# Causal attention and an MLP block on one NeuronCore: normalised rows of batches 2 to 5 turned by SyncE's transposing DMAs, MLP chunks begun two heads later

## The chip, the cores and the metric

The kernel runs on one core of one Trainium2 chip. The metric is the device time of one execution in microseconds. Before the change it is 359.73 us, the median of three runs (357.85 to 361.63).

## The reference

Eight batches with eight heads each, sequence 576, head size 64. First causal attention with a cumulative bias, then per row a layer norm and a two-layer MLP (512 to 2048 to 512) with a residual:

```python
scores = scale * np.matmul(q, k.transpose(0, 1, 3, 2))
s_pos = np.maximum(s, 0.0)
cum = np.cumsum(s_pos, axis=-1)
bias = -(cum[:, :, :, None] - cum[:, :, None, :])
scores = np.where(causal, -1000000000.0, scores + np.minimum(bias, 0.0))
attn = softmax(scores)                       # rows
x = np.matmul(attn, v)                       # heads side by side: (8, 576, 512)
mu, var = mean and variance of each row of x
xn = (x - mu) / np.sqrt(var + 1e-06) * g_ln
out = x + np.maximum(xn @ w_ch1, 0.0) @ w_ch2
```

## The kernel before, in words

All 64 (batch, head) pairs are numbered n = 8 b + h. TensorE computes, head by head, the transposed scores in three PSUM banks (`sa`, `sb`, `sc`, and `sd` for the last 64 rows of a pair of heads), ScalarE exponentiates them into `er`, GpSimd zeroes the part above the diagonal (`affine_select`), TensorE multiplies with the values into `pot` (`pv`, two heads behind), and VectorE divides by the row sums into `xb`, the fp32 rows of x (`pv_norm`). Rows 512 to 575 of two batches share one tile `xm`, so that an odd batch has five tiles of rows and an even one four.

Layer norm and MLP of a batch follow its attention. `ln_stats` takes the statistics in three parts as heads 3, 5 and 7 of the batch are finished; `ln_xn` writes the centred and scaled rows in bf16 (`xn`, the division by the deviation is left to the end, as `rstd`). These are turned into `xT` (features on partitions) in one of two ways. `ln_tr` has TensorE turn four 128x128 blocks into a PSUM bank of pool `ps_t` (tile `trx`), which VectorE or ScalarE copies out. `ln_tr_dma` has SyncE (SP) issue one transposing DMA from `xn` into `xT`. Constant `NXD` chooses: batches up to `NXD - 1` go through TensorE, the later ones through the DMA. Then a chunk of 32 units of MLP work is put into `queue`: 16 times `mlp1` (four matmuls of 512 columns into bank `ph`, ReLU into `hT`), and 16 times `mlp2` (four matmuls, a quarter of one row tile's output in `py`; after the fourth, VectorE writes `yo` and SP stores it). `ph` and `py` share the two PSUM banks of pool `ps_m`; the scores have three banks in `ps_s`. A ninth chunk does the shared row tiles (`xTm`).

The keys and queries of the first five groups of four heads (a group is called `gam` in the code, 0 to 15) come over other ways. From group 5 on, SP loads fp32 rows (`ld_rows`, ten transfers for a group, named `rowtmp`, line 175), GpSimd casts them into `rows`, a part of `kq[2]` (`cast_rows`, lines 192 and 195), and SP issues five transposing DMAs into `kq[0]` or `kq[1]` (`tr_rows`, line 208). `pre(n)` and `post(n)` hold the schedule: the loads of group g are placed at n = 4g-6, 4g-5 and 4g-4, the casts one head later, the transposes at 4g-4 and 4g-3, and the first use is at n = 4g. The values are loaded with a cast by GpSimd's own DMA queue (`ld_cast_v`). `pre(14)` has GpSimd write zeroes into columns 68 to 127 of the five `rows` tiles.

The order is written out by hand (`manual_schedule`): every engine runs its instructions in the order in which the program records them, and waits in it. SP's queue thus holds, in one line, row loads, transposes of keys and queries, transposes of `xn`, and stores of `yo`; a store that waits for its `yo` holds up everything recorded after it. The main loop (n = 18 to 63) records for each head its scores, one MLP unit, `post`, another unit, a finished head's `pv_next`, the layer norm steps of the batch before, and further units so that the chunk is used up by `end`, the head after which the next chunk is put in.

Of the kernel before, what the change touches and what calls it, by code (L numbers as in the profile page):

```python
# [9 lines left out]
F32 = mybir.dt.float32  # L10
# [5 lines left out]
P = 128  # L16
# [3 lines left out]
def kernel(  # L20
# [11 lines left out]
    nc = tc.nc  # L32
    B, H, S, D = q.shape
# [5 lines left out]
    NF = S // P  # L39
# [9 lines left out]
    NPE = 5  # L49
    NM = 10  # L50
    NHW = 16
    NXD = 6
    KT = 96
    QT = 6
    QP = S // QT
# [282 lines left out]
    def scores(b, h):  # L338
        e = er[:, h % 4, :]
        pe_mask = b * H + h < NM  # L340

        def bank(name, blocks, o):
            a = ps_s.tile([P, 512], F32, name=name, tag="s")
            for c, kb, q0, q1, diag in blocks:
                for a0, a1, cols in q_cols(b, h, q0, q1):
                    nc.tensor.matmul(  # L346
                        a[:, c + a0 - q0 : c + a1 - q0],
                        lhsT=k_cols(b, h, kb),
                        rhs=cols,
                        start=True,  # L350
                        stop=not (pe_mask and diag),
                    )
                if pe_mask and diag:
                    nc.tensor.matmul(
                        a[:, c : c + P], lhsT=ident, rhs=maskT, start=False, stop=True
                    )
            nc.scalar.activation(out=e[:, o : o + 512], in_=a, func=ACT.Exp, scale=scale)  # L357

        bank("sa", ((0, 0, 0, 512, True),), 0)
        bank("sb", ((0, 0, 512, 576, False), (64, 1, 128, 576, True)), OB)  # L360
        bank("sc", ((0, 2, 256, 576, True), (320, 3, 384, 576, True)), OC)
        if pe_mask:
            return
        for o, step in ((0, OB + 64), (OC, 320)):
            two = e[:, o : o + 2 * step].rearrange("p (i c) -> p i c", c=step)[:, :, 0:P]
            nc.gpsimd.affine_select(  # L366
                out=two,
                in_=two,
                compare_op=ALU.is_ge,
                fill=0.0,  # L370
                base=0,
                pattern=[[0, 2], [1, P]],
                channel_multiplier=-1,
            )
# [78 lines left out]
        return ts_  # L453

    st = {}

    def ln_stats(b, part):
        if part == 0:
            st[b] = small.tile([P, 5, 3, 6], F32, name="stats", tag="stats", bufs=2)
        lo, hi = ((0, 256), (256, 384), (384, 512))[part]  # L460
        for t, x in enumerate(x_tiles(b)):
            nc.vector.bn_stats(out=st[b][:, t, part, :], in_=x[:, lo:hi])  # L462

# [66 lines left out]

    def mlp1(xT, fb):
        on_dve = first_unit[0]
        ph = ps_m.tile([P, 512], F32, name="ph", tag="m")
        for kd in range(KD):
            nc.tensor.matmul(  # L537
                ph,
                lhsT=w1_bf[:, kd, fb * P : (fb + 1) * P],
                rhs=xT[:, kd, :],  # L540
                start=(kd == 0),
                stop=(kd == KD - 1),
            )
        if on_dve:
            nc.vector.tensor_scalar_max(out=hT[:, fb, :], in0=ph, scalar1=0.0)  # L545
        else:
            nc.scalar.activation(out=hT[:, fb, :], in_=ph, func=ACT.Relu)  # L547
# [22 lines left out]
    def chunk_units(xT_of, of_t, last=False):  # L570
        units = [lambda fb=fb: mlp1(xT_of(), fb) for fb in range(FB)]
        for t in range(NF):
            halves = ((0, 256), (256, 512)) if last and t == NF - 1 else ((0, 512),)
            for c in halves:
                for qr in range(4):
                    units.append(lambda t=t, qr=qr, c=c: mlp2(t, qr, *of_t(t), *c))
        return units
# [18 lines left out]
    def run_units(n, dve_first=False):  # L596
        for i in range(n):
            if queue:
                first_unit[0] = dve_first and i == 0
                queue.pop(0)()  # L600

# [24 lines left out]
    nc.vector.memset(v_bf[0][0:TL, NF, :, D : D + 1], 1.0)  # L628
    for i in range(2):
        nc.vector.memset(kq[i][0:KA, 0, :, S:SP], 0.0)  # L630
    nc.vector.memset(kq[2][0:KA, 0, :, S:SP], 0.0)
    nc.vector.memset(eight, 1.0 / scale)
    nc.vector.memset(mhalf, -0.5)
    nc.vector.memset(c3[BH:KT], 0.0)
# [22 lines left out]
    ld_cast_tile("q", NF)  # L657
    ld_cast_v(0, NF)

    for u, two in ((0, -1.0058441162109375), (1, 1.0019378662109375)):  # L660
        nc.gpsimd.memset(kq[2][D:KA, u].bitcast(F32)[:, :, 0 : S // 2], two)
    ld_w1(1)
    nc.gpsimd.memset(v_bf[1][:, 0:NF, :, D : D + 1], 1.0)
    nc.gpsimd.memset(v_bf[1][0:TL, NF, :, D : D + 1], 1.0)
# [185 lines left out]


    def pre(n):
        if n == 14:
            for r in rows:
                nc.gpsimd.memset(r[:, :, :, KA:P], 0.0)
        if n in PAIR_LOADS:
            ld_cast_pair(PAIR_LOADS[n])
        if n in (11, 12):
            ld_w2(n - 9)
        if n in (8, 9):  # L860
            aug(n - 5, nc.sync)
        for gam in range(NPE, NG):
            m = n - 4 * gam
            ts_ = {-6: (0, 1), -5: (2, 3), -4: (4,)}.get(m, ())
            for t in ts_:
                if gam < NHW:
                    ld_rows(gam, t)
                else:
                    ld_cast_rows(gam, t)
                    bias_of_rows(gam, t)  # L870
            if gam >= NHW:
                for t in {-4: (0, 1), -3: (2, 3, 4)}.get(m, ()):
                    tr_rows(gam, t)
        for nb in range(2, B):
            t = n - H * nb + (5 if nb == 2 else 6)
            if 0 <= t < NT:
                ld_cast_v(nb, t)

# [97 lines left out]
        STEPS[name](*args, *([E[eng]] if eng else []))  # L976

    pend += [(2, 0), (2, 1)]
    for n in range(2 * H + 2, BH):
        b, h = n // H, n % H  # L980
        pre(n)

        end = next(m for m in [8 * i + (3 if i <= NXD else 4) for i in range(2, B)] + [BH + 3] if m >= n)
        nu = -(-len(queue) // (end - n + 1)) - 2
        scores(b, h)
        run_units(1, True)
        if h % 2 == 0:
            scores_d(b, h // 2)
        post(n)
        run_units(1)  # L990
        pv_next()
        pend.append((b, h))
        if b <= NXD:
            if n == 2 * H + 2:
                for t in range(3, NT):
                    ln_xn(1, t)
            if b > 2 and h == 1:
                for t in range(NT):
                    ln_xn(b - 1, t)
            for t in {2: (0, 1), 3: (2, 3, 4)}.get(h, ()):  # L1000
                ln_tr(b - 1, t, "act" if b == 2 else "dve")
                if t != 1 and t != 4:
                    run_units(1)
                    nu -= 1
        elif h in (1, 2):
            for t in ((0, 1, 2), (3, 4))[h - 1]:
                ln_xn(b - 1, t)
                ln_tr_dma(b - 1, t)
                run_units(1)
                nu -= 1  # L1010
        run_units(nu)
        if n == end:
            run_units(len(queue))
            queue += batch_units(b - 1)
# [41 lines left out]
```

## Time and profile before

| | |
|---|---|
| median of three runs | 359.73 us (357.85 to 361.63) |
| the profiled execution: its own time | 358.78 us |
| its span, first to last instruction | 357.1 us |
| TensorE (PE) matmul rows busy | 349.3 us, 98% of the span |
| VectorE (DVE), ScalarE (ACT), GpSimd (POOL) busy | 196.2, 185.5, 162.2 us |
| SP's ring of the DMA queues (q1) | 116016 packets, 36.53 MB |
| granted TensorE clock | 1.000 |

A busy TensorE row holds the latency of a matmul too, and the rows of successive matmuls overlap; the rate is read from the starts of a run of them. "PEld" is the weight load, which overlaps the matmul. In the views an entry such as `[1.71 <-DMA kq<-kq]` tells how long the engine had been idle before an instruction and what released it.

### The profile page before, as it was taken

To read this page: it belongs to the slowest core of one execution; us is meant where nothing else is said; L and a number is where in the kernel's file an instruction comes from. 1 tells how busy PE (TensorE), PEld (TensorE's weight loads), DVE (VectorE), ACT (ScalarE), POOL (GpSimd) and SP (SyncE) were. 2 spreads that over 40 slices of the span, in tenths; PEclk is the share of its full clock that TensorE was granted. 3 is DMA by queue.
4 is the path that set the end of the run, shared out by engine and by line. 5 is a ranking of instruction groups with operands and counts; after the bars stand their busy time and mean duration, and the time that the engine had idled before them with its cause. 6 is when DMAs were issued, how large, how long until landed. Compare 5 with 4: busy or idle time off the path is not lost.

```text
span 357.1 us, 8417 instructions
## 1 busy us (share of the span) xinstructions
PE 349.3 (98%) x3154; PEld 198.9 (56%) x3154; DVE 196.2 (55%) x535; ACT 185.5 (52%) x359; POOL 162.2 (45%) x344
## 2 busy tenths in 40 slices
PE   8999999999899999999999999999999999999995
PEld 3899666555455555555565555555555544444444
DVE  7788888944376536844384539543764582113111
ACT  4899886577434763267336743475366403402500
POOL 9997669458436742582556452665341010000000
PEclk9999999999999999999999999999999999999999
DMA  9999999999979998699979974999740043011013
GB/s 151 170 180 171 199 190 166 191 192 168 184 147 204 153 212 149 106 226 172 171 129 213 207 145 84 222 180 174 158 119 2 0 80 113 0 61 60 0 32 89
DMA packets 169098, 49.73 MB, mean 139 GB/s; under 512 B 157744, under 2 KB 164448, under 8 KB 169056
## 3 DMA queue, kind: packets, MB, share of 16 engines
q1 hardware_dynamic: 116016, 36.53, 53.6%
q0 software_dynamic: 51600, 11.87, 37.1%
q10 hardware_dynamic: 1440, 0.79, 0.8%
q8 instruction: 25, 0.41, 0.5%
q14 instruction: 17, 0.14, 0.1%
HBM read 37.11 MB, written 9.44 MB: 130 GB/s over the span
## 4 chain that ended last, share of the span: by engine, by line
PE 84%; DVE 6%; DMA 3%; SPq 3%; POOL 2%; issue 1%; ACT 1%; DVEq 0%; POOLq 0%; ACTq 0%
PE py L555 31%; PE ph L537 29%; PE pot L424 6%; PE sc L346 3%; PE sb L346 3%; PE sa L346 3%; PE ph L817 2%; DVE xn L499 2%; DMA kq<-kq 2%; PE st L715 2%; SPq L175 1%; DMA rowtmp<-in_q_dram 1%; PE trx L526 1%; SPq L208 1%; PE pot L773 1%
## 5 line engine op out<-in xcount | busy, mean ns | idle before, releaser
L555 PE MATMUL py<-w_bf,hT 128*128 128x512 bf16 (+1 forms) x592 | 135.5, 373 | 0.4 <-DVE yo L564 0.4
L537 PE MATMUL ph<-xT,w_bf 128*128 128x512 bf16 x480 | 114.0, 379 | 0.0
L547 ACT ACTIVATE hT<-ph 128x512 bf16<-128x512 f32 x101 | 60.2, 597 | 74.3 <-PE ph L537 74.3
L555 PEld LDWEIGHTS <-hT 128*128 128x128 bf16 x592 | 53.7, 98 | 50.7 <-issue 0.9
L537 PEld LDWEIGHTS <-w_bf 128*128 128x128 bf16 x544 | 48.7, 97 | 50.5 <-issue 3.1
L366 POOL TENSOR_SCALAR_AFFINE_SELECT er<-er 128x256 bf16<-128x256 bf16 x108 | 43.7, 419 | 53.2 <-ACT er L357 52.3
L357 ACT ACTIVATE er<-sa 128x512 bf16<-128x512 f32 x56 | 33.3, 595 | 64.9 <-PE sa L346 50.3
L545 DVE TENSOR_SCALAR hT<-ph 128x512 bf16<-128x512 f32 x35 | 24.2, 692 | 57.3 <-PE ph L537 52.4
L192 POOL CAST kq<-rowtmp 128x512 bf16<-128x512 f32 (+1 forms) x55 | 33.5, 609 | 29.3 <-DMA rowtmp<-in_q_dram 27.4
L346 PEld LDWEIGHTS <-kq 68*128 68x128 bf16 x412 | 29.7, 97 | 23.5 <-DMA kq<-kq 2.0
L424 PEld LDWEIGHTS <-er 128*128 128x128 bf16 x840 | 32.8, 98 | 11.9
L436 DVE RECIPROCAL rinv<-pot 128x5 f32<-128x5 f32 x56 | 10.7, 192 | 50.0 <-PE pot L424 49.8
L564 DVE SCALAR_TENSOR_TENSOR yo<-py,rstd,xb 128x512 f32<-128x512 f32 x32 | 24.0, 749 | 24.2 <-PE py L555 19.5
L424 PE MATMUL pot<-v_bf,er 128*128 128x65 bf16 x840 | 34.7, 194 | 0.0
L165 POOL DMA_DIRECT2D v_bf<-in_v_dram x40 | 34.4, 867 | 0.3 <-DVE kq L116 0.3
L357 ACT ACTIVATE er<-sb 128x512 bf16<-128x512 f32 x56 | 33.5, 598 | 1.3 <-PE sb L346 1.3
L357 ACT ACTIVATE er<-sc 128x512 bf16<-128x512 f32 x56 | 34.1, 610 | 0.0
L478 POOL TENSOR_TENSOR rstd<-rstd,mhalf 128x4 f32<-128x4 f32 (+1 forms) x8 | 8.9, 1115 | 45.0 <-DVE rstd L477 45.0
L438 DVE TENSOR_TENSOR xb<-pot,rinv 128x256 f32<-128x256 f32 x56 | 23.8, 424 | 1.9
L346 PE MATMUL sb<-kq 68*128 68x64 bf16 (+1 forms) x156 | 21.4, 241 | 1.7 <-DMA kq<-kq 1.7
L462 DVE BATCH_NORM_STATS2 stats<-xb 128x6 f32<-128x128 f32 (+1 forms) x84 | 21.9, 320 | 0.3
L346 PE MATMUL sc<-kq 68*128 68x256 bf16 (+1 forms) x200 | 21.7, 226 | 0.1
(116 smaller groups left out, 354.2 us busy)
## 6 DMA issues: line engine op xcount, KB each, us to landing
out_dram<-yo SPq DMA_DIRECT2D x32, 256.0 KB
rowtmp<-in_k_dram SPq DMA_DIRECT2D x44, 128.0 KB
rowtmp<-in_q_dram SPq DMA_DIRECT2D x44, 128.0 KB
v_bf<-in_v_dram POOLq DMA_DIRECT2D x32, 128.0 KB, 6.1
w_bf<-in_moe_w_ch_dram POOLq DMA_DIRECT2D x8, 512.0 KB, 9.1
kq<-kq SPq DMA_TRANSPOSE x55
kp<-in_k_dram POOLq DMA_DIRECT2D x6, 144.0 KB, 8.7
qp<-in_q_dram POOLq DMA_DIRECT2D x6, 144.0 KB, 8.8
```

Source lines behind the costliest of these rows:

```text
L165: nc.gpsimd.dma_start(out=v_bf[b % 2][:pn, t, :, 0:D], in_=v[b, :, t * P : t * P + pn, :].rearrange("h s d -> s h d"),)
L192: nc.gpsimd.tensor_copy(out=rows[t][0:pn, :, :, 0:D], in_=loaded.pop(("rows", gam, t))[0:pn])
L346: nc.tensor.matmul(a[:, c + a0 - q0 : c + a1 - q0], lhsT=k_cols(b, h, kb), rhs=cols, start=True, stop=not (pe_mask and diag),)
L357: nc.scalar.activation(out=e[:, o : o + 512], in_=a, func=ACT.Exp, scale=scale)
L366: nc.gpsimd.affine_select(out=two, in_=two, compare_op=ALU.is_ge, fill=0.0, base=0, pattern=[[0, 2], [1, P]], channel_multiplier=-1,)
L424: nc.tensor.matmul(pot[:, t, :], lhsT=e[:, o : o + P], rhs=vv[:, kb, h, :], start=(kb == 0), stop=(kb == last),)
L438: nc.vector.tensor_tensor(out=xb[b][:, :, hs], in0=pot[:, 0:NF, 0:D], in1=rinv[:, 0:NF].unsqueeze(2).to_broadcast([P, NF, D]), op=ALU.mult,)
L537: nc.tensor.matmul(ph, lhsT=w1_bf[:, kd, fb * P : (fb + 1) * P], rhs=xT[:, kd, :], start=(kd == 0), stop=(kd == KD - 1),)
L545: nc.vector.tensor_scalar_max(out=hT[:, fb, :], in0=ph, scalar1=0.0)
L547: nc.scalar.activation(out=hT[:, fb, :], in_=ph, func=ACT.Relu)
L555: nc.tensor.matmul(py[t], lhsT=hT[:, fb, t * P : (t + 1) * P], rhs=w2_bf[:, fb, c0:c1], start=(fb == 0), stop=(fb == FB - 1),)
L564: nc.vector.scalar_tensor_tensor(out=yo, in0=py[t], scalar=rs, in1=x[:, c0:c1], op0=ALU.mult, op1=ALU.add)
```

## The change

- `NXD` goes from 6 to 2: the rows of batches 2 to 5 (18 row tiles) are turned by SP's transposing DMAs instead of 72 TensorE transposes and 18 VectorE copies. `XN_AT` places the steps: at the batch's h = 1 three tiles are normalised and two transposes issued, at h = 2 two and two, at h = 4 the transpose of the shared tile.
- The chunks of batches 2 to 6 enter the queue after h = 5 instead of h = 3 (batch 6: h = 4) of the batch that follows. Chunk 1 therefore spreads over heads 20 to 29 instead of 20 to 27, and `FIRST` puts two units ahead of the scores of head 24.
- `ln_stats` no longer records its instructions at once: they go into `todo`, and two of them are recorded after each MLP unit; part 2 and batches 0 and 1 still go at once.
- The `ph` banks of the last two chunks come from pool `ps_s`.
- The last row tile of the last chunk is computed in three pieces (256, 128 and 128 columns) instead of two of 256.
- The zeroes in `kq[2]`: one VectorE memset at the start and the five of `pre(14)` go; GpSimd writes one more near the start and two over more partitions. The values of batch 3 are loaded two heads later.

```diff
--- before.py
+++ after.py
@@ -49,7 +49,7 @@
     NPE = 5
     NM = 10
     NHW = 16
-    NXD = 6
+    NXD = 2
     KT = 96
     QT = 6
     QP = S // QT
@@ -453,13 +453,22 @@
         return ts_
 
     st = {}
+    todo = []
+
+    def run_todo(n):
+        for _ in range(min(n, len(todo))):
+            todo.pop(0)()
 
     def ln_stats(b, part):
         if part == 0:
             st[b] = small.tile([P, 5, 3, 6], F32, name="stats", tag="stats", bufs=2)
         lo, hi = ((0, 256), (256, 384), (384, 512))[part]
         for t, x in enumerate(x_tiles(b)):
-            nc.vector.bn_stats(out=st[b][:, t, part, :], in_=x[:, lo:hi])
+            todo.append(
+                lambda t=t, x=x: nc.vector.bn_stats(out=st[b][:, t, part, :], in_=x[:, lo:hi])
+            )
+        if part == 2 or b < 2:
+            run_todo(len(todo))
 
 
 
@@ -532,7 +541,8 @@
 
     def mlp1(xT, fb):
         on_dve = first_unit[0]
-        ph = ps_m.tile([P, 512], F32, name="ph", tag="m")
+        late = xT not in list(xTs.values())[0 : B - 1]
+        ph = (ps_s if late else ps_m).tile([P, 512], F32, name="ph", tag="s" if late else "m")
         for kd in range(KD):
             nc.tensor.matmul(
                 ph,
@@ -570,7 +580,7 @@
     def chunk_units(xT_of, of_t, last=False):
         units = [lambda fb=fb: mlp1(xT_of(), fb) for fb in range(FB)]
         for t in range(NF):
-            halves = ((0, 256), (256, 512)) if last and t == NF - 1 else ((0, 512),)
+            halves = ((0, 256), (256, 384), (384, 512)) if last and t == NF - 1 else ((0, 512),)
             for c in halves:
                 for qr in range(4):
                     units.append(lambda t=t, qr=qr, c=c: mlp2(t, qr, *of_t(t), *c))
@@ -598,6 +608,7 @@
             if queue:
                 first_unit[0] = dve_first and i == 0
                 queue.pop(0)()
+                run_todo(2)
 
 
 
@@ -628,7 +639,6 @@
     nc.vector.memset(v_bf[0][0:TL, NF, :, D : D + 1], 1.0)
     for i in range(2):
         nc.vector.memset(kq[i][0:KA, 0, :, S:SP], 0.0)
-    nc.vector.memset(kq[2][0:KA, 0, :, S:SP], 0.0)
     nc.vector.memset(eight, 1.0 / scale)
     nc.vector.memset(mhalf, -0.5)
     nc.vector.memset(c3[BH:KT], 0.0)
@@ -657,8 +667,9 @@
     ld_cast_tile("q", NF)
     ld_cast_v(0, NF)
 
+    nc.gpsimd.memset(kq[2][:, :, :, S:SP], 0.0)
     for u, two in ((0, -1.0058441162109375), (1, 1.0019378662109375)):
-        nc.gpsimd.memset(kq[2][D:KA, u].bitcast(F32)[:, :, 0 : S // 2], two)
+        nc.gpsimd.memset(kq[2][D:P, u].bitcast(F32)[:, :, 0 : S // 2], two)
     ld_w1(1)
     nc.gpsimd.memset(v_bf[1][:, 0:NF, :, D : D + 1], 1.0)
     nc.gpsimd.memset(v_bf[1][0:TL, NF, :, D : D + 1], 1.0)
@@ -850,9 +861,6 @@
 
 
     def pre(n):
-        if n == 14:
-            for r in rows:
-                nc.gpsimd.memset(r[:, :, :, KA:P], 0.0)
         if n in PAIR_LOADS:
             ld_cast_pair(PAIR_LOADS[n])
         if n in (11, 12):
@@ -872,7 +880,7 @@
                 for t in {-4: (0, 1), -3: (2, 3, 4)}.get(m, ()):
                     tr_rows(gam, t)
         for nb in range(2, B):
-            t = n - H * nb + (5 if nb == 2 else 6)
+            t = n - H * nb + {2: 5, 3: 4}.get(nb, 6)
             if 0 <= t < NT:
                 ld_cast_v(nb, t)
 
@@ -976,12 +984,17 @@
         STEPS[name](*args, *([E[eng]] if eng else []))
 
     pend += [(2, 0), (2, 1)]
+    XN_AT = {1: ((0, 1, 2), (0, 1)), 2: ((3, 4), (2, 3)), 4: ((), (4,))}
+    FIRST = {24: 2}
     for n in range(2 * H + 2, BH):
         b, h = n // H, n % H
         pre(n)
 
-        end = next(m for m in [8 * i + (3 if i <= NXD else 4) for i in range(2, B)] + [BH + 3] if m >= n)
+        end = next(m for m in [8 * i + (3 if i <= NXD else 5) for i in range(2, B)] + [BH + 3] if m >= n)
         nu = -(-len(queue) // (end - n + 1)) - 2
+        if n in FIRST:
+            run_units(FIRST[n])
+            nu -= FIRST[n]
         scores(b, h)
         run_units(1, True)
         if h % 2 == 0:
@@ -994,20 +1007,24 @@
             if n == 2 * H + 2:
                 for t in range(3, NT):
                     ln_xn(1, t)
-            if b > 2 and h == 1:
-                for t in range(NT):
-                    ln_xn(b - 1, t)
+            for t in {1: (0, 1, 2), 2: (3, 4)}.get(h, ()) if b > 2 else ():
+                ln_xn(b - 1, t)
+                if t in (1, 2, 4):
+                    run_units(1)
+                    nu -= 1
             for t in {2: (0, 1), 3: (2, 3, 4)}.get(h, ()):
                 ln_tr(b - 1, t, "act" if b == 2 else "dve")
-                if t != 1 and t != 4:
+                if t not in (1, 4) and nu > 0:
                     run_units(1)
                     nu -= 1
-        elif h in (1, 2):
-            for t in ((0, 1, 2), (3, 4))[h - 1]:
+        elif h in XN_AT:
+            for t in XN_AT[h][0]:
                 ln_xn(b - 1, t)
+                if t != 1 and nu > 0:
+                    run_units(1)
+                    nu -= 1
+            for t in XN_AT[h][1]:
                 ln_tr_dma(b - 1, t)
-                run_units(1)
-                nu -= 1
         run_units(nu)
         if n == end:
             run_units(len(queue))
```

## The prediction

> **What bounds the kernel now.** First the page's busy times and DMA queues: is one engine nearly always at work, and what else is full?
>
> ```profile
> PE 349.3 (98%) x3154; PEld 198.9 (56%) x3154; DVE 196.2 (55%) x535; ACT 185.5 (52%) x359; POOL 162.2 (45%) x344
> ...
> q1 hardware_dynamic: 116016, 36.53, 53.6%
> ```
>
> TensorE is the bound, but 98% could hide slow stretches, so I read its rate from the chain of work that ended last, in order of time (start, length, what):
>
> ```profile
> 284.62 12.09 PE py L555 x56
> 296.71 14.49 PE ph L537 x64
> 311.20 13.86 PE py L555 x64
> 325.05 14.31 PE ph L537 x64
> ```
>
> 56 matmuls in 12.09 us are 0.216 us each, the `py` run of 64 in 13.86 us as well: full rate. The two `ph` runs of the last chunks take 0.63 and 0.45 us more for the same 64. Time leaves this kernel in two ways only: fewer TensorE columns, or fewer of its few holes. TensorE's timeline shows what a transpose costs and the two larger kinds of hole:
>
> ```profile
> 71.01 0.39 PE L526 MATMUL trx<-ident,xn 128*128 128x128 bf16 x4
> 72.10 0.61 PE L526 MATMUL trx<-ident,xn 128*128 128x128 bf16 x8
> ```
> ```profile
> 93.08 0.39 PE L346 MATMUL sb<-kq 68*128 68x64 bf16 x3 [1.71 <-DMA kq<-kq]
> ```
> ```profile
> 145.34 0.39 PE L346 MATMUL sc<-kq 68*128 68x256 bf16 x4
> 145.94 1.89 PE L555 MATMUL py<-w_bf,hT 128*128 128x512 bf16 x8 [0.21 <-DVE yo L564]
> ```
>
> Eight transposes take 0.61 us and four 0.39: (0.61 - 0.39) / 4 = 55 ns each (the 219 ns mean in the groups is mostly latency). Head 24 begins at 91.00 and its second bank waits for the keys of group 6 until 93.08; undisturbed it begins some 0.22 later than the first (145.12 against 144.90 at head 35), so about 1.87 us are lost. At 145.5 a `py` bank is late because VectorE did five `xn` first; the same stands at 221.6. `sc` could have been followed after 0.22, so each costs 0.38 us.
>
> Last, SP's queue, where the transposes go (timeline of SP, around a batch's heads 1 to 4):
>
> ```profile
> 136.76 4.00 SPq L208 DMA_TRANSPOSE kq<-kq  x3
> 145.91 0.36 SPq L582 DMA_DIRECT2D out_dram<-yo  x1
> 146.32 0.43 SPq L175 DMA_DIRECT2D rowtmp<-in_k_dram  x1
> ...
> 255.23 2.51 SPq L518 DMA_TRANSPOSE xT<-xn  x2
> ```
>
> Its last transpose of keys ends at 140.8; then SP stands still until 145.9 at a store whose `yo` isn't there. A transpose of `xn` holds it 1.25 us (two in 2.51). The DMA share (second last column) of the stretch 142 to 145 says that the rings are empty too:
>
> ```profile
> 142.00:145.00 3.00, 3.00 (x35) 1.87 (x33) 2.89 (x8) 0.01 (x1) 0.00 (x0) 1.00 0.00 0
> ```
>
> **The change, part by part.**
>
> *TensorE transposes.* 18 tiles of 4, 72 x 55 ns = **-4.0 us**. All stands on TensorE's path. The 18 VectorE copies of 0.416 us go too; VectorE is 55% busy, so that counts only through the next item.
>
> *The two late `yo`.* The chunk now begins after h = 5, so at h = 1, when the `xn` are made, TensorE does `ph` units, which ScalarE empties, and the five `xn` are split 3 and 2 with units between. Both holes go: 2 x 0.38 = **-0.75**. If the split isn't enough they stay: 0.
>
> *The statistics spread, `FIRST`.* Same VectorE instructions in other places, 0, hidden in VectorE's 45% of idle time; without that cover, a delayed `yo` of the 0.38 kind for each of five batches, +1.9. `FIRST` moves two units of 0.86 us from after head 22 and 23's work to just before head 24; counted in the order of instructions, TensorE reaches head 24 after the same number of columns as before: 0.
>
> *Banks for the last chunks.* `ph` gets three banks of its own instead of two that it shares with `py`: the excess of 0.63 + 0.45 us goes, I take **-1.0** (between 0 and -1.1). No scores are left that need them.
>
> *The three last pieces.* 32 matmuls of 128 columns for 16 of 256: at 55 ns each, as the transposes of 128 columns show, against 0.109, the same TensorE time. The last `yo` is shorter: 0.75 us for 512 columns, 0.48 for 256, so some 0.35 for 128: -0.13. One VectorE memset of 0.17 us leaves the start, where VectorE's memsets run up to 4.49 and the bias chain starts at 4.52: -0.12. Together **-0.25**.
>
> *GpSimd.* 2.25 us of memsets (53.95, five) leave the stretch in which GpSimd runs without a break up to the casts of group 5; one of about 0.5 us is added near 16 us, before the loads of weights that TensorE doesn't wait for. The value loads of batch 3 move two heads back, so the two that GpSimd issued at 63.70 and 72.38, in front of and beside group 6's row loads (71.2 to 80.8), no longer compete with these. So groups 5 and 6 come earlier by up to 2.25 us and the hole of 1.87 at head 24 shrinks; I take **-1.4** (between 0 and -1.87).
>
> *SP.* 18 more transposes of 1.25 us: 22.5 us of SP time, 5.6 for a batch of five tiles. Behind each wait the row loads of the next group, behind these GpSimd's casts, SP's own transposes, and TensorE's scores. In a steady batch (heads 32 on) I cost them at nothing. What hides them is the hole above: SP stands 5.1 us before the store at h = 2, the stores now come at h = 2 to 5, later, and the transposes fill the place. First loads of the next group at 146.3 before; after: wait for the second `xn` until about 142, two transposes to 144.5, loads from 144.5. Group 10's last transpose is issued at 161.8 and head 40 begins at 168.9. One in a full ring landed 6.07 us after its issue (the chain's step into head 24, from 86.97), one in an emptying ring within 2.6 (issued at 102.4, no DMA busy from 105 on), so 1 to 4.5 us are to spare. Without the hole, +0.9 a batch: SP was not held at a store for about 32.2 of 38 us, 32.2 + 5.6 = 37.8, and TensorE now takes 36.9 for a batch (38 less transposes and holes).
>
> A rule against this change: the Trainium skill, "VectorE: DVE Perf Modes", sections "The three transpose paths" and "Rules for kernel authors", gives 390 ns for a 128x128 bf16 block on TensorE and 1309 ns for the DMA crossbar, and advises TensorE where the result may go to PSUM. By its figures the 72 blocks would take 28 us off TensorE and put 94 us on the DMA path, and the steady batches would stall. The trace has 55 ns and a quarter of 1.25 us, and the sum goes by these.
>
> *Heads 24 to 32.* Here the cover is thinnest. Chunk 1 is thinned, so in the order of instructions heads 24 to 29 hold 64 MLP matmuls instead of 96 and no 16 transposes: 32 x 0.216 + 16 x 0.055 = 7.8 us sooner at head 30, while DMA work per head grows. Group 8, needed at head 32: before, SP issued its five transposes at 117.4 to 126.0, and head 32 began at 130.6. After, head 32 would begin near 121 (130.6 - 1.87 - 7.8). SP ends group 7's transposes at about 101 (they hang on casts recorded behind head 25, no sooner), then a store, two `xn` transposes, four loads, a store, two transposes, six loads and a store: 0.5 + 2.5 + 2.2 + 0.5 + 2.5 + 3.4 + 0.5 gives 113; the last load lands and is cast some 6 us after its issue (107.07 to 113.22 in the trace, first load to cast), about 118.5, and the last transpose is issued near 119.5 and lands 2.6 to 6.1 us later. So TensorE waits between 1 and 5 us; nearer the emptying ring, since SP's next loads come behind a store that waits: **+2.5**. Bounds: 0 if SP runs 2 us earlier, 6 with one more blocked store (3 us at 103.7). Group 7's last transpose, issued near 99.5, lands at 102 to 105.6; head 28 begins near 105: no wait that counts.
>
> *Sum:* -4.0 - 0.75 - 1.0 - 0.25 - 1.4 + 2.5 = **-4.9 us**. On the profiled execution's 358.78 that is 353.9. This execution lies 0.95 below the median of the three runs; I take the middle, 359.25, as the time before: **354.4 us**.
>
> **The rivals.**
>
> 1. *No new wait at all.* Head 24's hole vanishes and head 32 waits for nothing: -4.0 - 0.75 - 1.1 - 0.25 - 1.87 = -8.0, so 351.3. For it: the loads land faster once two value loads have left. Against: the sum of group 8 above.
> 2. *The gain goes into keys that come late.* 5 us at head 32, 0.9 in each of three steady batches and the hole of head 24 unchanged: -6.0 + 5 + 2.7 = +1.7, and -1.0 if the steady batches don't lose: 358.3 to 361.0, middle 359.6. For it: the page has DMA at 9 tenths in most slices up to 260 us, and transposes next to other traffic took up to 2.55 us (the longest of line 518). Against: the rings' own hole at 142 to 145.
> 3. *SP becomes the bound: slower.* If a transpose of `xn` holds SP for 2 us on average (between the median of 1.22 and the longest of 2.55) and the place of the blocked store isn't gained, a batch takes 32.2 + 4.5 x 2 = 41.2 us of SP against TensorE's 36.9: 4.3 x 4 batches = 17, less 6.0 of gains: +11, 370. It decides from (32.2 + 4.5 c) > 36.9 + 6.0/4, that is c > 1.4 us. For it: 1.25 isn't far from 1.4. Against: of the 32.2 us about 7 are SP waiting for room in full rings, which shorten when work is spread.
>
> **How the numbers follow.** Forecast 0.53, rival 1 0.16, rival 2 0.18, rival 3 0.13. About 1% (3.6 us) is what a measurement of this kernel can tell from no change. The likeliest case reaches from 351.9 (head 32 free) to 357.9 (6 us there). Rival 1 lies just below and is taken in with 0.8 us for the scatter of the runs; at the top the range goes to 359.5, the middle of rival 2, and leaves out the other half of it and rival 3: 350.5 to 359.5. Faster by over 1% (below 356.1): rival 1 and 0.50 of the forecast, 0.66; within 1%: the rest of the forecast and rival 2, 0.21; slower: rival 3, 0.13.
>
> **What would show it.** Right: no `trx` row after head 19, 3.96 us fewer TensorE columns; no `py` row with a hole from VectorE at h = 2; `ph` runs of 64 in 13.9 us; at head 24 less than 1 us and at head 32 1 to 5 us of idle time released by `kq<-kq`; SP's row loads for a batch's group 2b+2 starting as far ahead of their head as before. Wrong: several holes by `kq<-kq` at heads 36 to 60 (rival 3), `ph` waiting for an `xT` that hasn't landed when a chunk begins, or a PE span that shrinks by less than the 4 us of columns with the holes elsewhere.

## The result, and the profile after

The changed kernel takes 362.3 us (median of 20 runs, 359.6 to 366.6) beside 358.4 for the kernel before on the same chip: a ratio of 1.0100, 95% interval 1.0079 to 1.0120, 3.6 us slower. The ratio leaves out four of the 20 runs, slow ones that lie over 1.5% above the quickest, and is therefore smaller than the quotient of the medians. The forecast was 354.4. The profiled execution, 359.56 us, is the quickest of the 20, so it shows less of the loss than the median has; e1 below, the same kernel but for one memset, was profiled at 362.25 and stands for the usual run.

First the page of after: the busy times, the granted TensorE clock in 40 slices, and SP's ring (packets, MB, share).

```profile
PE 345.9 (97%) x3098; PEld 195.4 (55%) x3098; DVE 190.6 (53%) x516; ACT 186.3 (52%) x360; POOL 162.7 (45%) x340
...
PEclk9999999899999999999999999999999999999999
...
q1 hardware_dynamic: 125888, 38.89, 58.8%
```

TensorE is busy 3.4 us less (the forecast had 4.0 us of columns less), yet the time has not followed: the share fell to 97%. The chain of work that ended last shows that the tail did what was forecast (start, length, what):

```profile
284.85 13.81 PE py L565 x64
298.67 13.81 PE ph L547 x64
312.48 13.81 PE py L565 x64
326.29 13.81 PE ph L547 x64
340.11 10.37 PE py L565 x48
```

Both `ph` runs are now as quick as `py`. The waits of TensorE (us in total, times, longest) name what took the gain:

```profile
PE sa L346 <- DMA kq<-kq: 2.6, 1, 2.6
PE py L565 <- DMA w_bf<-in_moe_w_ch_dram: 2.6, 2, 2.2
```

TensorE's timeline has them behind the scores of head 17 (first row) and at head 32 (last row); between them the two rows of head 24, which no longer waits:

```profile
63.21 1.86 PE L565 MATMUL py<-w_bf,hT 128*128 128x512 bf16 x4 [2.19 <-DMA w_bf<-in_moe_w_ch_dram]
...
95.83 0.38 PE L346 MATMUL sa<-kq 68*128 68x512 bf16 x1
96.05 0.38 PE L346 MATMUL sb<-kq 68*128 68x64 bf16 x3
...
128.70 0.38 PE L346 MATMUL sa<-kq 68*128 68x512 bf16 x1 [2.63 <-DMA kq<-kq]
```

Head 24 begins 4.8 us later than before (91.00), while the last key transpose of its group was issued at 86.93 us (before: 86.97). So its hole is gone because TensorE comes late, not because the keys come early.

The table by windows shows that the hole of 2.19 us cost twice. Columns: window, length, busy time and count of PE, PEld, DVE, ACT, POOL, granted clock, DMA share (the time of all packets, divided by the window and by 16 engines), GB/s.

```profile
60.00:64.00 4.00, 1.81 (x22) 1.05 (x21) 1.67 (x4) 1.60 (x4) 2.69 (x8) 0.85 1.86 133
64.00:68.00 4.00, 4.00 (x33) 2.15 (x32) 1.87 (x4) 2.26 (x3) 0.76 (x2) 0.72 1.42 130
```

These are means; in windows of one microsecond the granted clock is 0.50 from 63 to 66 us. TensorE works again from 63.21 on, so this costs some 3 x 0.5 = 1.5 us more. Before, both windows have 1.00.

Last SP's queue in the batch that the prediction looked at, heads 34 to 40:

```profile
141.49 2.65 SPq L527 DMA_TRANSPOSE xT<-xn  x2
144.19 0.58 SPq L175 DMA_DIRECT2D rowtmp<-in_k_dram  x1
...
146.51 0.45 SPq L592 DMA_DIRECT2D out_dram<-yo  x1
147.00 2.81 SPq L527 DMA_TRANSPOSE xT<-xn  x2
149.85 0.58 SPq L175 DMA_DIRECT2D rowtmp<-in_k_dram  x1
...
157.88 1.29 SPq L527 DMA_TRANSPOSE xTm<-xn  x1
159.26 0.54 SPq L592 DMA_DIRECT2D out_dram<-yo  x1
159.91 4.53 SPq L208 DMA_TRANSPOSE kq<-kq  x3
```

From 141.49 to 165.12 SP is issuing for 22.4 of 23.6 us. Three of the five transposes stand between the first row load (144.19) and the last key transpose (issued 163.21, head 40 at 165.74). I call the time from the issue of a group's last key transpose to the start of its first head its *lead*. For groups 8, 10, 12 and 14 the leads were 5.8, 7.1, 7.4 and 5.9 us before and are 3.0, 2.5, 2.8 and 3.7 after.

### The profile page after: what moved, and what is told of

Same layout as the page of the kernel before. It is cut to its first block, busy times and chain, and to the rows that moved or that the text cites. A ratio compares the mean times of both kernels' runs of the same rounds, so it can differ in the third digit from the quotient of the medians.

```text
span 357.9 us, 8328 instructions
## 1 busy us (share of the span) xinstructions
PE 345.9 (97%) x3098; PEld 195.4 (55%) x3098; DVE 190.6 (53%) x516; ACT 186.3 (52%) x360; POOL 162.7 (45%) x340
## 4 chain that ended last, share of the span: by engine, by line
PE 80%; DMA 11%; POOL 5%; ACT 2%; DVE 1%; issue 1%; SPq 0%; DVEq 0%; ACTq 0%; POOLq 0%
PE py L565 33%; PE ph L547 29%; PE pot L424 6%; DMA w_bf<-in_moe_w_ch_dram 4%; PE sb L346 3%; PE sa L346 3%; PE sc L346 3%; DMA v_bf<-in_v_dram 2%; DMA kq<-kq 2%; DMA tiletmp<-in_k_dram 1%; POOL v_bf L165 1%; ACT er L357 1%; DMA out_dram<-yo 1%; POOL er L366 1%; POOL kq L672 1%
## 5 line engine op out<-in xcount | busy, mean ns | idle before, releaser
L565 PE MATMUL py<-w_bf,hT 128*128 128x512 bf16 (+2 forms) x608 | 135.8, 370 | 2.6 <-DMA w_bf<-in_moe_w_ch_dram 2.6
L366 POOL TENSOR_SCALAR_AFFINE_SELECT er<-er 128x256 bf16<-128x256 bf16 x108 | 44.7, 430 | 43.6 <-ACT er L357 42.8
L346 PE MATMUL sa<-kq 68*128 68x512 bf16 x56 | 21.3, 381 | 2.7 <-DMA kq<-kq 2.6
L508 DVE SCALAR_TENSOR_TENSOR xn<-xb,mv,gb 128x512 bf16<-128x512 f32 x28 | 21.9, 783 | 1.0
```

What stands on the lines that cost most here:

```text
L346: nc.tensor.matmul(a[:, c + a0 - q0 : c + a1 - q0], lhsT=k_cols(b, h, kb), rhs=cols, start=True, stop=not (pe_mask and diag),)
L366: nc.gpsimd.affine_select(out=two, in_=two, compare_op=ALU.is_ge, fill=0.0, base=0, pattern=[[0, 2], [1, P]], channel_multiplier=-1,)
L565: nc.tensor.matmul(py[t], lhsT=hT[:, fb, t * P : (t + 1) * P], rhs=w2_bf[:, fb, c0:c1], start=(fb == 0), stop=(fb == FB - 1),)
```

## The experiments

The letters of theories hold within an expectation, not from one to the next. Each ratio is against the kernel before, run on the same chip; times are medians. The edits are against after unless another kernel is named.

### GpSimd's added memset

GpSimd's weight loads start 0.92 us later, 0.55 of it by the memset; the transfer ahead of the memset was already 0.36 later (timeline of GpSimd, before and then after):

```profile
17.84 0.77 POOL L220 DMA_DIRECT2D w_bf<-in_moe_w_ch_dram  x1
```
```profile
16.15 0.55 POOL L670 MEMSET kq<- 128x512 bf16 x1
...
18.76 0.77 POOL L220 DMA_DIRECT2D w_bf<-in_moe_w_ch_dram  x1
```

The last block of weights landed at 59.59 before and at 63.17 after, so this was the first suspect.

**e1_pad_on_vector**: the zeroes are written by VectorE.

```diff
+    nc.vector.memset(kq[2][:, :, :, S:SP], 0.0)
     nc.vector.memset(eight, 1.0 / scale)
...
-    nc.gpsimd.memset(kq[2][:, :, :, S:SP], 0.0)
```

> The changed kernel with one edit undone: the padding columns of kq[2] are zeroed by VectorE at the start, as before, and not by GpSimd (0.55 us, in front of the second block of the first MLP weights in GpSimd's queue). Theory W (the weight stream comes late because of that memset): the holes at 36 (0.50 us), 56.5 (0.57) and 60.8 (2.35), and the 1.2 us at a lower clock after them, go; 362.3 falls to about 357 (355.5 to 358.5), and the last block of the second weights lands near 60 instead of 63.2. Rival H (the keys of group 8 at head 32 are what makes it slow, and the start varies by itself): no more than 0.6 us, 361.5 to 362.5. Either way the 2.8 us hole at head 32 stays.

362.0 us, ratio 1.0102 (1.0059 to 1.0144): nothing is won, as rival H said. In the profiled runs, which are not alike (after's is its quickest), the weights' hole is 1.0 us instead of 2.6, and others stand in its place:

```profile
PE sa L346 <- DMA kq<-kq: 4.7, 2, 3.0
...
PE ph L547 <- DMA xT<-xn: 1.0, 1, 1.0
PE py L565 <- DMA w_bf<-in_moe_w_ch_dram: 1.0, 1, 1.0
```

The two holes by keys are at heads 32 and 56, and after the one at head 32 the clock falls:

```profile
124.00:126.00 2.00, 0.23 (x2) 0.00 (x0) 0.42 (x3) 0.60 (x1) 0.44 (x2) 1.00 1.43 181
126.00:128.00 2.00, 0.77 (x7) 0.42 (x8) 0.00 (x0) 0.35 (x1) 0.00 (x0) 1.00 0.98 249
128.00:130.00 2.00, 2.00 (x12) 0.92 (x11) 0.53 (x1) 1.50 (x4) 0.24 (x1) 0.65 0.94 213
130.00:132.00 2.00, 2.00 (x19) 1.27 (x18) 0.36 (x2) 0.60 (x1) 1.18 (x4) 0.50 0.96 217
```

Four microseconds at 0.58 on average cost another 1.7 us (4 x 0.42).

**e2_before_pad_on_gpsimd**: the kernel before, with the memset alone moved to GpSimd.

```diff
-    nc.vector.memset(kq[2][0:KA, 0, :, S:SP], 0.0)
...
+    nc.gpsimd.memset(kq[2][:, :, :, S:SP], 0.0)
```

> The kernel before with that edit alone: the padding of kq[2] zeroed by GpSimd ahead of the second weight block, the VectorE memset gone. Theory W: holes of some 2 to 4 us by the weights near head 17 and a lower clock after them; 358.4 rises to 361 to 363.5. Rival H: within 0.6 us of before.

359.5, ratio 1.0045 (1.0023 to 1.0067): the memset by itself costs about 1.6 us (0.0045 x 358), less than theory W and more than rival H had; the profiled run has a hole of 1.5 by late weights. But the memset is not the only thing that makes the weights late. With it on VectorE the profiled runs have from none (e4) to 1.1 us (e12) of that hole, and e8 below, whose instructions up to this place are those of before, has 1.4. So why taking the memset out of after wins nothing stays open.

### Thin heads, and batch 2

A head is called thin where fewer MLP units stand between its scores and the next head's.

**e3_chunk1_nine_heads** (against e1): chunk 1 is used up one head earlier (heads 20 to 28, in before 20 to 27), so that heads 24 to 28 are fuller than in e1.

```diff
-        end = ... [8 * i + (3 if i <= NXD else 5) for i in range(2, B)] ...
+        end = ... [8 * i + {2: 3, 3: 4}.get(i, 5) for i in range(2, B)] ...
```

> e1 with chunk 1 spread over heads 20 to 28 instead of 20 to 29 (chunk 2 begins after head 28). Theory T (the hole at head 32 comes because heads 24 to 29 are thin and TensorE arrives 7.8 us sooner): it reaches head 32 some 4 us later, the 2.8 us hole goes, 2 to 3 us less than e1, about 354. Rival S (SP's transposes of batch 2's rows delay group 8 and what follows): the hole turns up again at head 36 or as a wait for xT; within 1 us of e1.

364.65, ratio 1.0210 (1.0154 to 1.0265), slower still. Head 32's hole is nearly gone (0.35), but chunk 2 begins before its `xT` has landed (2.1 us of wait). Chunk 2 now takes nine heads (29 to 37) instead of eight, so that the thinner heads lie ahead of head 40, where TensorE waits 3.8 us for keys and then has a clock of 0.50 up to 172 us. Moving the MLP work moves the hole; it doesn't remove it.

**e4_batch2_on_tensor** (against e1): batch 2's rows are turned by TensorE again; batches 3 to 5 stay with SP.

```diff
-    NXD = 2
+    NXD = 3
...
-        end = ... (3 if i <= NXD else 5) ...
+        end = ... (3 if i <= 2 else 5) ...
```

> e1 with the rows of batch 2 alone turned on TensorE again (16 transposes, 0.9 us; SP has four transposes of 1.25 us less between heads 25 and 28), chunks unchanged. Theory T: head 32 still waits 1 to 2 us; e1 - 0.5 to + 0.5. Rival S: the hole at head 32 goes entirely; 1.5 to 2 us less than e1.

357.43, ratio 0.9955 (0.9923 to 0.9988), faster than both kernels. 4 of the 18 transposes thus decide 0.0147 x 358.4 = 5.3 us (e1 and e4 ran on the same chip), where theory S had 1.5 to 2. What e1's profile shows at batch 2 agrees: 1.0 for `xT`, 2.95 at head 32 and 1.7 by the clock are 5.7 us. The waits for keys in e4 (one profiled run, the quickest):

```profile
PE sb L346 <- DMA kq<-kq: 0.9, 2, 0.7
PE sa L346 <- DMA kq<-kq: 0.5, 1, 0.5
```

1.2 of these 1.4 us are at head 24, where `xn` transposes play no part; at head 32 0.2 are left.

### The order of SP's work

**e5_even_loads_early** (against e1) and **e6_batch2_tensor_even_early** (the same against e4): the row loads of even groups are placed one head earlier.

```diff
         for gam in range(NPE, NG):
             m = n - 4 * gam
+            m += gam >= 8 and gam % 2 == 0
```

> e1 with the row loads of the even groups from 8 on (heads 32, 40, 48, 56) put one head earlier in SP's queue, ahead of the xn transposes; nothing else moved, the same transfers in all. Theory S (what SP issues between an even group's loads, the third to fifth xn transpose, is what makes that group late): the holes at heads 32, 40, 48 and 56 (3.3, 0.2, 0.7 and 2.3 us in e1, and the lower clock after the first) go, 362.0 falls to 355 to 357. Rival D (the DMA rings are full, the order doesn't matter): the holes stay or move to the odd groups, within 1.5 us of e1.

> e4 (batch 2's rows on TensorE) with the same earlier loads. S: the rest of e4's holes goes and the runs lie closer together: 354 to 355.5 against 357.4. D: no better than e4.

e5: 363.75, ratio 1.0162 (1.0092 to 1.0232), with seven waits for keys (6.4 us together), now for odd groups too (2.0 at head 28). e6: 361.25, ratio 1.0030 (0.9979 to 1.0081), with seven waits of 4.8 us where e4 had three of 1.4. Earlier loads don't help; the leads of the odd groups pay, 3.7 to 5.3 us in e5 for groups 9 to 13 where e1 has 7.3 to 8.7.

**e10_row_loads_first** (against e1) and **e11_batch2_tensor_loads_first** (the same against e4): all ten row loads stand ahead of the transposes of `xn`.

```diff
+            if gam >= 8 and gam % 2 == 0:
+                ts_ = {-6: (0, 1), -5: (2, 3, 4)}.get(m, ())
...
-    XN_AT = {1: ((0, 1, 2), (0, 1)), 2: ((3, 4), (2, 3)), 4: ((), (4,))}
+    XN_AT = {1: ((0, 1, 2), ()), 2: ((3, 4), ()), 3: ((), (0, 1, 2, 3)), 5: ((), (4,))}
```

> e1_pad_on_vector with another order in SP's queue and nothing else: all ten row loads of an even group (from group 8 on) stand ahead of the batch's transposes of xn (four of these together after the head h = 3, the shared tile's after the group's five key transposes), the last row load one head earlier. Theory O (order): the keys come late because the row loads begin behind the xn transposes and the casts' and landings' latency stands idle afterwards; now SP turns the xn while the rows land and are cast, so the even groups' last transposes come 3 us earlier against the heads: holes at heads 32, 40, 48, 56 below 0.5 us each, 356 to 358.5 (against 362.0). Rival R (amount): SP and its ring simply have 5 us more to do in each batch, wherever it stands: the last key transposes are as late as before, holes of 1 us or more at two of these heads or at a chunk's first ph by xT, 360.5 to 363.

> e4_batch2_on_tensor (357.43, batch 2's rows on TensorE, batches 3 to 5 by SP) with the same order as e10_row_loads_first. Theory O: the remaining holes by keys (heads 32 to 56) go, 354 to 356.5, faster than before by 0.6 to 1.2%. Rival R: as e4 or slower, 357 to 360.

e10: 363.81, ratio 1.0128 (1.0046 to 1.0210). Its holes by keys shrink to 0.8 us, and the chunks' first `ph` waits instead. SP issued the four transposes at 110.0 to 115.4, TensorE wanted the result at 112.6:

```profile
110.01 5.35 SPq L527 DMA_TRANSPOSE xT<-xn  x4
```
```profile
118.76 1.01 PE L547 MATMUL ph<-xT,w_bf 128*128 128x512 bf16 x2 [6.13 <-DMA xT<-xn]
```

e11: 357.71, ratio 0.9976 (0.9948 to 1.0005), as e4. No order tried makes room: what SP does later, something waits for. That speaks for the amount, not the order.

### The amount: SP's time or the traffic

**e7_before_extra_transposes** and **e8_before_extra_copies_act** leave the kernel before whole and add work to it: 18 transposes of the same `xn` by SP into a tile that nobody reads, or 18 copies of the same size in pieces of 256 bytes by ScalarE's queue.

```diff
+            for t in {1: (0, 1), 2: (2, 3), 4: (4,)}.get(h, ()) if b > 2 else ():
+                if (b - 1, t) in kept:
+                    nc.sync.dma_start_transpose(      # e8: nc.scalar.dma_start, at h = 2 to 4
+                        out=extra[:, :, t % 2 * P : (t % 2 + 1) * P], in_=kept.pop((b - 1, t))
+                    )
```

> The kernel before, all its TensorE transposes kept, with the 18 xn transposes of batches 2 to 5 issued by SP as well, at the changed kernel's places (h = 1, 2 and 4), into a spare tile that nothing reads. S: the even groups come some 4 us later; holes by kq<-kq at heads 32, 40, 48 and 56 of 0 to 3 us each: 358.2 rises by 1 to 5. D: the same, since the traffic is the same. If nothing moves (within 0.7 us), the transposes cost nothing by themselves and it is the chunks' place that matters (theory C).

> As e7, but the 18 tiles are copied, not transposed, into the spare tile in pieces of 256 bytes, and ScalarE's queue issues them: the traffic without SP's time. S: within 0.7 us of before, or well under half of e7's loss. D: the loss of e7.

e7: 360.62, ratio 1.0052 (1.0020 to 1.0083); leads of groups 8 to 14 (even) 4.2, 2.9, 5.4 and 3.8. e8: 360.28, ratio 1.0038 (1.0014 to 1.0063); leads 6.2, 5.9, 6.5 and 4.7, and no wait for keys. In these two profiles the leads are taken by SP's time more than by the traffic: group 10 loses 4.2 us in e7 and 1.2 in e8. But the copies aren't transposes and stand at other heads, and the times hardly differ. e8's waits are elsewhere: 1.4 us for weights at 61 us, ahead of all its copies, and 1.3 for a ReLU of ScalarE. The extra tile also shifts other tiles in memory, so the cost in us isn't settled by this pair; e7's profiled run took 365.34 us, so that only its leads are used.

**e9_all_batches_on_tensor** (against e1): everything of the change but the SP transposes.

```diff
-    NXD = 2
+    NXD = 6
...
-        end = ... (3 if i <= NXD else 5) ...
+        end = ... (3 if i <= 2 else 5) ...
```

> Everything of the change except its main part: the rows of batches 2 to 5 are turned by TensorE again (72 transposes, 18 VectorE copies), while the chunks still begin at the sixth head, with the spread steps, the spare banks and the pad on VectorE as in e1_pad_on_vector (362.0). Theory Q (the 18 transposes in SP's queue are what costs): TensorE gets 4.0 us more work, but the holes by keys at heads 32, 40 and 56 and by xT at 114 go (in e1 3.3, 0.2, 2.3 and 1.2 us, with some 2 us at a lowered clock): 355.5 to 358, that is 2 to 4 us below e1, no hole by keys over 0.7 us from head 28 on. Rival P (the later place of the chunks costs: thin heads 24 to 29 and stores that come later in the batch): head 32's hole stays at 2 us or more, and the time is 361 to 364.

357.35, ratio 0.9966 (0.9933 to 0.9999). With 72 more transposes on TensorE it is faster than e1 by 0.0136 x 358.4 = 4.9 us. The leads of groups 10, 12 and 14 are 8.0, 7.5 and 7.0. This is SP's queue without them, in the same batch:

```profile
137.37 0.57 SPq L175 DMA_DIRECT2D rowtmp<-in_k_dram  x1
...
141.75 0.36 SPq L592 DMA_DIRECT2D out_dram<-yo  x1
...
150.29 0.89 SPq L592 DMA_DIRECT2D out_dram<-yo  x1
151.29 5.62 SPq L208 DMA_TRANSPOSE kq<-kq  x3
```

The first row load comes 25.7 us ahead of head 40 (at 163.09); in after it comes 21.5 ahead, in before 22.6. So the later chunks did clear the hole in front of the store, by 3.1 us; the first two transposes then use it up, and one more microsecond.

**e12_transposes_by_scalar** (against e1) and **e14_batch2_tensor_rest_by_scalar** (the same against e4): ScalarE's queue issues them.

```diff
-            nc.sync.dma_start_transpose(out=xT_dst(b, t), in_=xns.pop((b, t)))
+            (nc.scalar if b < B - 2 else nc.sync).dma_start_transpose(...)
...
+    XN_AT = {1: ((0, 1, 2), ()), 2: ((3, 4), (0,)), 3: ((), (1, 2)), 4: ((), (3,)), 5: ((), (4,))}
```

> e1_pad_on_vector (362.0) with the 18 transposes of xn of batches 2 to 5 issued by ScalarE's queue instead of SP's, spread over the heads h = 2 to 5 of a batch. The traffic in the DMA engines is the same, SP's queue is that of e9_all_batches_on_tensor, TensorE has its 72 transposes less. Theory Q1 (what costs is SP's time: 1.25 us for each transpose in the one line in which row loads, stores and key transposes stand): the even groups' leads return to the 7 us of e9, no hole by keys over 0.7 us from head 40 on, and the time is that of e9 less the 4 us of TensorE, with up to 2 us lost to exponentials that stand behind ScalarE's transposes: 353.5 to 356. Rival Q2 (what costs is the traffic in the DMA engines, from whichever queue): leads of 2.5 to 5 us and holes as in e1, 359.5 to 363.

> e4_batch2_on_tensor (357.43) with the 14 transposes of batches 3 to 5 issued by ScalarE instead of SP. Theory Q1: no hole by keys over 0.5 us from head 40 on, TensorE saves 56 transposes or 3.1 us against e9: 353.5 to 355.5. Rival Q2: as e4, 357 to 359.

380.8 and 376.3, ratios 1.0655 (1.0595 to 1.0715) and 1.0469 (1.0392 to 1.0546), which neither theory foresaw. ScalarE's timeline in e12:

```profile
153.75 0.60 ACT L357 ACTIVATE er<-sc 128x512 bf16<-128x512 f32 x1
164.22 1.21 ACTq L527 DMA_TRANSPOSE xTm<-xn  x1
165.52 0.60 ACT L357 ACTIVATE er<-sa 128x512 bf16<-128x512 f32 x1 [11.17 <-issue]
```

ScalarE stands 9.9 us ahead of one transpose, with the exponentials of the next head behind it. By the semaphores in the trace it waits there for the key transposes that SP issued at 156.98, 158.36 and 160.60; the last of them landed at 164.15. So this pair tells nothing of SP's time against the traffic; that question rests on e7 and e8.

### A third of them, and where they stand

**e13_half_by_sync** (against e9): tiles 0 and 1 of batches 3, 4 and 5 go by SP.

```diff
-                ln_tr(b - 1, t, "act" if b == 2 else "dve")
+                if b > 3 and t < 2:
+                    ln_tr_dma(b - 1, t)
+                else:
+                    ln_tr(b - 1, t, "act" if b == 2 else "dve")
```

> e9_all_batches_on_tensor (357.35) with tiles 0 and 1 of batches 3, 4 and 5 turned by SP (6 transposes, after the second head of the batch that follows), the other tiles and the whole of batch 2 by TensorE. Theory Q (SP has a fixed spare time in a steady batch, the even groups' lead of 7 to 8 us in e9 less the 3 to 5 us of a landing, so 3 to 4 us): 2.5 us for a batch fit, leads of 4.5 to 5.5 us, no hole by keys over 0.4 us at heads 40 to 56, and TensorE saves 24 transposes of 55 ns, 1.3 us: 355.5 to 356.8. Rival F (each transpose costs by itself, in proportion; e1 lies 4.65 above e9 for 18): 6 of them bring +1.5, 358.5 to 359.5.

357.35, ratio 0.9965 (0.9935 to 0.9996), equal to e9. No wait for keys is left, as theory Q said, and the leads hardly fall (7.3, 7.7, 6.6; theory Q had 4.5 to 5.5), but the 1.3 us don't show in the median. The profiled run (357.36) has values 1.5 and weights 0.9 us late instead, so the two runs don't separate the 1.3 us from what happens at the start.

**e15_start_as_before_half_by_sync** (against e13) puts memsets, value loads and chunk 1 back to where before has them, so that the thin heads are 28 to 37 instead of 24 to 29; **e16_start_as_before_all_on_tensor** is the same without SP's six transposes.

```diff
-            t = n - H * nb + {2: 5, 3: 4}.get(nb, 6)
+            t = n - H * nb + (5 if nb == 2 else 6)
...
-    FIRST = {24: 2}
+    FIRST = {}
...
-        end = ... (3 if i <= 2 else 5) ...
+        end = ... (3 if i <= 3 else 5) ...
```

> A candidate for the better version: of the change it keeps the spare banks, the three last pieces, the spread statistics and split xn steps, and chunks from the sixth head for batches 3 to 6; as in before are GpSimd's and VectorE's zeroes, the value loads of batch 3, chunk 1 over eight heads (its end at head 27) and no units ahead of head 24; tiles 0 and 1 of batches 3, 4 and 5 go by SP, all others by TensorE (e13_half_by_sync had 357.35). Theory E (the 2 us that e9 and e13 lack against the terms of the prediction are lost before head 33: late weights and values at 60 to 70 us from the moved GpSimd work, and keys at head 32 from the thin heads 24 to 29): holes at 60 to 70 us below 0.5 us in sum, at head 24 up to 1.9 as in before, at head 32 below 0.4: 354.5 to 356.5. Rival N (those holes come and go from run to run whatever stands in the queues): 356.5 to 358.5, no different from e13.

> e15_start_as_before_half_by_sync with all tiles of batches 2 to 5 on TensorE, so that the two tell what six of SP's transposes are worth once more: 24 TensorE transposes of 55 ns more, 1.3 us. Theory Q (six fit into SP's spare time): 1.0 to 1.5 us above e15. Rival F (each costs as much as it saves or more): equal to e15 within 0.5 us, or below it.

e15: 363.1, ratio 1.0135 (1.0102 to 1.0169). e16: 357.03, ratio 0.9983 (0.9960 to 1.0007). Six transposes, free in e13, cost 0.0152 x 358.2 = 5.4 us here. The place is head 40, behind the thin heads (TensorE's timeline, then SP's):

```profile
165.18 0.59 PE L346 MATMUL sa<-kq 68*128 68x512 bf16 x1 [4.01 <-DMA kq<-kq]
```
```profile
144.32 2.53 SPq L527 DMA_TRANSPOSE xT<-xn  x2
...
153.35 9.18 SPq L208 DMA_TRANSPOSE kq<-kq  x5
```

In e16 group 10 has a lead of 5.7 us without any transpose of `xn`. SP's time is only a part of what takes it in e15: behind the two transposes the next row loads are issued 3.1 us later than in e16 (146.90 against 143.83), but the cast that waits for them starts 5.5 us later (154.47 against 148.99). GpSimd's timeline, and the window in which the DMA engines moved 29 GB/s, in e16 208:

```profile
154.47 0.61 POOL L192 CAST kq<-rowtmp 128x512 bf16<-128x512 f32 x1 [5.01 <-DMA rowtmp<-in_q_dram]
```
```profile
148.00:150.00 2.00, 2.00 (x23) 1.14 (x20) 0.81 (x3) 0.58 (x2) 1.45 (x4) 1.00 1.93 29
```

Why the loads landed so late isn't shown. Behind the hole the clock is 0.50 for over six microseconds. e15's start shows no late weights (theory E was right there), yet e16 isn't faster than e9.

## Why the prediction was wrong, point by point

By medians and ratios the 3.6 us divide as follows (each ratio is uncertain by 0.2 to 0.4%, about 1 us):

| part | from | predicted | measured |
|---|---|---|---|
| all but SP's transposes, the memset on VectorE | e9 | -3.4 | -1.2 |
| 14 transposes, batches 3 to 5 | e4 against e9 | -3.1 | -0.4 |
| 4 transposes, batch 2 | e1 against e4 | -0.9 + 2.5 = +1.6 | +5.3 |
| the memset on GpSimd, in after | after against e1 | 0 | -0.1 |
| sum | | -4.9 | +3.6 |

- **TensorE's columns (-4.0): right.** The last `trx` row starts at 77.37 us, ahead of head 20 (77.42), and TensorE has 72 x 128 = 9216 columns less, 3.9 us at 0.216 us for 512.
- **The two late `yo` (-0.75) and the banks (-1.0): right in after's trace.** No `py` waits for VectorE, and the two `ph` runs take 13.81 us each instead of 14.49 and 14.31.
- **GpSimd (-1.4): not earned, though the sign that I named came true.** Head 24 waits for nothing in after, by luck: TensorE is 4.8 us late there. Where TensorE comes on time the hole is still there: in e4, which has GpSimd's other moves, head 24 waits 0.5 and 0.7 us and its second bank starts at 92.85, in before at 93.08. In e9 it starts at 93.09. I also costed the added memset at nothing because TensorE "doesn't wait for" those weights. It does wait, for their last blocks at 60 us: 1.6 us by e2. I had looked only at what stands directly behind the memset, not at the end of the queue it delays (with the reservation above that late weights have other causes too).
- **SP in the steady batches (0): the first step that failed, by 2.7 us.** The store's hole was there and the chunks' shift cleared it (e9: first load 3.1 us earlier). But it took in two of four or five transposes. The other two or three (2.8 and 1.3 us) stand between the first row load and the last key transpose, and I had counted only the start of the loads. From first load to last key transpose it takes 15.5 us before and 19.0 after. With heads that come sooner because TensorE does less, 7.1 us of lead became 2.5, and there "1 to 4.5 us to spare" was none. In after's quickest run the steady batches wait less than 0.4 us at any head; in e1 it is 1.8 us at head 56. The 14 transposes bring 0.4 us of the 3.1 by the medians; no profile shows the missing 2.7 us whole, e4's being of its quickest run.
- **Head 32 (+2.5): right in place, wrong in size; with 3.7 us the largest error.** After's profile has a hole of 2.63 us there, e1's 2.95. That this is so near to 2.5 is partly luck: the last key transpose was issued at 125.70 and not near 119.5, and TensorE was ready at 126.07 and not near 121. And batch 2's transposes cost more than the hole: `xT` came 1.0 us late for chunk 2 in e1, and behind the idle 2.95 us the clock was lowered, 1.7 us in e1. The term was +5.3 + 0.9 = 6.2, against the bound of 6 that I gave it.
- **The rest of the change (-3.4, measured -1.2): not fully explained.** 1.4 of the missing 2.2 us is GpSimd's term. e9's profiled run also has keys 0.9 and 0.2 us late at head 32, and weights 0.7 late. e16, which starts as before, has neither; there VectorE's copy of `xT` is 0.9 us late (`trx` at 143.79). The rest is within the uncertainty.
- **The rivals.** Rival 2 (the gain goes into late keys, 358.3 to 361.0) names the mechanism that happened and ends 1.3 us too low; it had neither the lowered clock nor the late weights. Rival 3 (SP as the bound) had SP full, as the trace has it, but at the 1.25 to 1.4 us for a transpose that I took, not at 2.

What the runs show is one cause, the `xn` transposes in SP's queue, with a price that depends on the place: 14 or 6 cost about what they save where a group's lead without them is 7 us or more, and 4 or 6 cost 5 us where the heads ahead of it are thin (e1 against e4, e15 against e16). That it is SP's time alone is not shown: the leads of e7 and e8 speak for it, the late landing in e15 speaks for the DMA engines as well.

The best version run is e4, 0.9955 of the time before (0.9923 to 0.9988), with e9 and e13 not to be told from it: the change without batch 2's transposes on SP and without GpSimd's memset.

## What to carry to other kernels

A queue with a hole has not that much spare time: count, for the transfer that is needed first, everything that is put between its inputs' load and its own issue, and take off what the consumer gains on the other side, because a consumer made faster shortens the cover of its own supply. Work that is moved to such a queue is priced at the place with the smallest lead, not by an average batch; where the work of other engines was thinned at the same place, look there first. And one profiled run of a kernel with small leads is not typical of it: here it was the quickest of 20, and the loss was in the others.

## What the hardware showed that was not expected

- **The clock after a short idle time.** TensorE idle for 2.95 us (e1, head 32), 3.83 (e3, head 40) and 4.01 (e15, head 40) was followed by a granted clock of 0.50, for over three microseconds in e1 and over six in the two others. The hole in e1 so cost some 4.6 us (2.95 and 1.7). The length of the idle time alone doesn't tell: 2.63 us in after (head 32) were followed by 1.00, 1.56 in e5 (head 32, at 127.4 us) and 1.66 in e10 (at 196.7 us) by 0.50, and so were two holes of 0.41 and 2.19 within seven microseconds in after.
- **Transposes from two queues.** With key transposes on SP and `xn` transposes on ScalarE, ScalarE stood up to 9.9 us ahead of one in e12 (154.35 to 164.22 us), until the third of SP's had landed (164.15).
- **When a transpose lands.** In e10 the fourth of four transposes was issued at 114.09 us, and the matmul that waited for them started at 118.76; SP's issue time of 1.3 us says little of that.
